# The third channel block's forward transform in 128x128 matmuls, with the whole kernel put in a new order

## Chip, core and metric

The kernel runs on one core of a Trainium2 chip. The metric is the device time of one execution in microseconds; before the change it is 645.85 us, the median of three runs (645.35 to 647.2).

## The reference

One layer of a conditioned network on 2048 tokens of 640 channels, in float32: a gated long convolution, then a wide MLP.

```python
def _A_ref(q, k, v, shift_k, ssm_k, ssm_D):
    ...                                   # k_shift: causal convolution of k with 4 taps
    kv = k_shift * v
    L = 2 * S
    kv_f = rfft(pad(kv)); kf_f = rfft(pad(ssm_k))
    y = irfft(kv_f * kf_f, L)[:S]         # long causal convolution, per channel
    y = y + kv * ssm_D
    return q * y

def _B_ref(x, w1, b1, w2, b2):
    r = relu(x @ w1 + b1)
    return (r * r) @ w2 + b2

mod = silu(c) @ w_mod                     # six rows: sa, ca, ga, sb, cb, gb
h = layernorm(x) * (1 + ca) + sa
x = x + ga * _A_ref(h, A_k, A_v, A_shift_k, A_ssm_k, A_ssm_D)
h = layernorm(x) * (1 + cb) + sb
x = x + gb * _B_ref(h, B_w1, B_b1, B_w2, B_b2)
```

(S is 2048, the MLP's inner width 1728. The names of the transforms are shortened here.)

## The kernel before

**Two halves.** The first half works through the 640 channels in five blocks of 128 (b = 0 to 4): short convolution and product k * v, the long convolution as a Fourier transform of 4096 points done by matmuls, the gate. The second half is the MLP, in four groups of 512 tokens for its first layer and eight of 256 for its second, with products split into float32r terms.

**A channel block.** `kv` (line 642) turns a tile of k and of v (groups "kt", "vt" on TensorE, the tiles kva and kvb), applies the taps and stores kv to a scratch tensor in HBM, from which `load_x` brings it back in another layout, the tile p; `load_h` brings the filter. `unit_a` (712) is the first transform, "pa": for the filter (i = 1) and for the data (i = 0), in four units (n) of eight columns of p each. `spectra` does the second step ("h" and "x", the tiles a and gb), `front` (778) multiplies the spectra, `back` (806) is the first step of the inverse transform ("qp", the table gi, the tiles wxa and wxb), and `unit_y` (831) the second ("t", transposes of q, and "y", products with cst). `prep` and `finish` are the gate and the sum. `mod_row` and `mod_col` compute rows of the conditioning ("mr"); `awake` (700) puts in twenty dummy groups of transposes ("warm").

**Two forms of the first transform.** In `unit_a` a unit is 32 products of 64x64 quarters of the array: for each of eight columns, two halves e of the partitions and two halves r of the result. They are written as two half units of 16 products. A float32 product is two weight loads and two matmuls in the trace, so a unit is 64 matmuls, and 128 instructions. `unit_a4` (736), used where (b, i) is in the set FOUR, takes all 128 partitions at once, with a table cw4 of four columns in place of two:

```python
mm(
    t[64 * r : 64 * r + 64, j].rearrange("p m d -> p (m d)"),
    pt[b][:, i, 8 * n + 4 * half + j, :],
    cw4[:, r],
    True, True, hold=[AX[b][i]],
)
```

Here a unit is 16 products, 32 matmuls and 64 instructions. Both forms fill two PSUM tiles of 128x512 in a unit, and each is copied into the tile a ("pac"), in blocks 1 to 4 by ScalarE. Before the change FOUR holds blocks 0 and 1.

**The order.** Nothing is emitted where it is written. Every step becomes a node of a graph with a key, such as ("pa", 2), and the table TURNS (1419) gives each key's nodes their due times, in hundredths of a microsecond, in the order in which they were written; `order` (179) sorts all nodes by them, and `keep_order` pins each engine to that order. The due times are a planner's; here they count as an order and nothing else. HOMES (1878) gives, by one digit a tile, which of its allowed buffers or PSUM banks a tile lives in. `sp_issue` (408) holds a transfer on SyncE's queue (SP) until the fourth one ahead of it has landed.

Of the kernel before, what the change touches and what calls it, by code (L numbers as in the profile page):

```python
# [260 lines left out]
def ssm_mlp_kernel(  # L261
# [52 lines left out]
    warm = sb.tile([P, 1], F32, tag="warm", name="warm")  # L314
# [556 lines left out]
    st2 = small("st2", (P, 2, NB, 6))  # L871
# [484 lines left out]
    def second_layer(n):  # L1356
# [46 lines left out]
        def gated(i, k, t, done=True):  # L1403
# [16 lines left out]
        ("b1", 0): [6247, 21762],  # L1420
        ("comb", 0): [4983, 5176, 5350, 5419, 5488, 5213, 5281, 5524, 5705, 5636, 5774, 6000, 6069, 6207, 6138, 6286,
            6355, 6509, 6440],
        ("comb", 1): [9572, 9677, 9608, 9503, 9856, 9787, 9719, 10175, 9949, 10244, 10313, 10454, 10689, 10892, 10824,
            11060, 10961, 11790, 11721],
        ("comb", 2): [14697, 14661, 14802, 14593, 14940, 14871, 14733, 15045, 14976, 15396, 15186, 15327, 15563,
            16040, 16309, 16788, 16423, 16492, 16719],
        ("comb", 3): [18943, 19048, 18979, 19084, 19153, 19386, 19189, 19815, 19603, 19677, 19746, 20239, 20308,
            20453, 20384, 20627, 20696, 21071, 21002],
        ("comb", 4): [23016, 23179, 23284, 22947, 23586, 23215, 23435, 23622, 24236, 23901, 24098, 24304, 24167,
# [20 lines left out]
        ("fin", 0): [13154, 15631, 13193, 14121, 12280, 12414, 13259, 13393, 11593, 12714],  # L1450
        ("fin", 1): [14229, 18629, 18157, 17429, 15841, 16312, 14429, 14923, 16109, 16243],
        ("fin", 2): [18118, 19837, 21611, 18515, 18388, 18637, 18555, 19040, 19258, 19392],
        ("fin", 3): [22111, 23723, 23079, 22071, 23970, 24104, 23691, 25536, 24712, 25085],
        ("fin", 4): [25708, 25775, 25747, 26588, 26097, 26231, 26371, 26504, 26840, 27968],
        ("gb", 0): [1955, 2141, 2424, 1791],
        ("gi", 0): [5076, 5015, 4786, 4907],
        ("h", 1): [5206, 5951, 7416, 8020, 9524, 9622, 9719, 9816, 10092, 10205, 10282, 10386, 10457, 10554, 10662,
            10945],
        ("h", 2): [12405, 12587, 12824, 13274, 14536, 14648, 14726, 14823, 14901, 14998, 15274, 15387, 15377, 15767,
            15940, 16087],  # L1460
        ("h", 3): [17094, 17387, 18492, 18624, 18928, 19026, 19154, 19251, 19359, 19467, 19762, 20038, 20248, 20369,
            20428, 20529],
        ("h", 4): [21852, 21974, 22479, 22739, 22933, 23030, 23108, 23205, 23368, 23466, 23984, 24082, 24159, 24257,
            24334, 24592],
        ("hat", 0): [25954, 26016],
        ("hat", 1): [27079, 27284],
        ("hat", 2): [27688, 27782],
        ("hat", 3): [29066, 28707],
        ("hat", 4): [34016, 34515],
        ("hat", 5): [34703, 34910],  # L1470
        ("hat", 6): [36793, 37348],
        ("hat", 7): [38305, 38447],
# [426 lines left out]
    kn = {}  # L1899
# [139 lines left out]
```

## Time and profile before

| | |
|---|---|
| timed runs | 645.35, 645.85, 647.2 us |
| profiled execution | 650.69 us, of which the span 648.9 us |
| mean granted clock of TensorE | 0.987 |
| TensorE, matmuls | 623.3 us busy |
| VectorE | 501.7 us |
| ScalarE | 363.0 us |
| GpSimd | 209.8 us |
| data moved | 111.04 MB, mean 171 GB/s |

The profile is of one execution. PE is TensorE with its matmuls, PEld its weight loads, DVE VectorE, ACT ScalarE, POOL GpSimd, SP SyncE. A row of the timeline gives start, length, engine, line, operation, the tile written and the tiles read, shapes and count, and in brackets the idle time ahead of it with what ended it. A row of a table by stretches gives the stretch and its length, then each engine's busy time and instructions, then the granted clock of TensorE, the busy share of the DMA engines and GB/s. All steps bear the line of one helper (L195), so groups are told apart by their tiles: products with cst and p are the first transform, "64*64" its quarter form and "128*64" the other. "issue" is time in which an engine waited for nothing that the profile shows.

### The profile page before, as it was taken

The page shows a single profiled execution, that of the slowest core. Times are in us where ns is not written, and L with a number is a line of the kernel's source. Part 1 is how long each engine was busy: PE and PEld are TensorE (multiplying, and loading weights), DVE is VectorE, ACT ScalarE, POOL GpSimd, SP SyncE. Part 2 cuts the span into 40 slices and gives each one's busy share as a digit, 9 for nine tenths or more (in the row PEclk, how much of TensorE's full clock was granted, in tenths as well). Part 3 has the DMA queues.
Part 4 walks back from the last instruction along what each step waited for, and adds up shares of the span by engine and source line. Part 5 has one row for each costly group of instructions (what it writes and reads, how often), then busy time and mean ns, then how long its engine had stood idle before and what let it go on. Part 6 is the DMA issues. An engine that isn't in the chain of part 4 may idle for free.

```text
span 648.9 us, 17839 instructions
## 1 busy us (share of the span) xinstructions
PE 623.3 (96%) x7268; PEld 584.2 (90%) x7268; DVE 501.7 (77%) x970; ACT 363.0 (56%) x693; POOL 209.8 (32%) x284
## 2 busy tenths in 40 slices
PE   7999889989899899999999999999999999999997
PEld 7999579859878779689999899999999999999996
DVE  2659657877779658997877696776899898789886
ACT  3674665885756673566656756457894233423331
POOL 4338437767557518312334310105320000000000
PEclk9999989999989889999999999999999999999999
DMA  9799999889779722665565643144654445463633
GB/s 226 221 263 270 256 278 210 199 212 216 189 166 223 192 80 57 169 190 173 160 191 157 181 147 106 61 142 139 204 180 155 119 128 157 140 194 94 189 112 97
DMA packets 144714, 111.04 MB, mean 171 GB/s; under 512 B 51188, under 2 KB 123700, under 8 KB 144632
## 3 DMA queue, kind: packets, MB, share of 16 engines
q1 hardware_dynamic: 142500, 109.29, 61.3%
q8 instruction: 57, 0.93, 0.6%
q10 hardware_dynamic: 2068, 0.61, 0.4%
q14 instruction: 25, 0.20, 0.1%
q0 software_dynamic: 64, 0.01, 0.0%
HBM read 79.99 MB, written 29.88 MB: 169 GB/s over the span
## 4 chain that ended last, share of the span: by engine, by line
PE 81%; DMA 7%; DVE 5%; issue 3%; ACT 2%; POOL 1%; SPq 0%; DVEq 0%; POOLq 0%
PE ps L195 81%; DMA q<-in_A_q_dram 3%; DMA wm<-in_w_mod_dram 2%; DVE kva L195 1%; DMA d<-in_A_ssm_D_dram 1%; DMA w2s<-in_B_w_dram 1%; DMA kvb<-in_A_k_dram 1%; DVE w L195 1%; DVE s L195 1%; ACT xf L195 0%; DVE xf L195 0%; POOL kacc L195 0%; DVE up L195 0%; DVE outs L195 0%; DVE kacc L195 0%
## 5 line engine op out<-in xcount | busy, mean ns | idle before, releaser
L195 PEld LDWEIGHTS ps<-a,gb 128*64 128x64 f32 x1260 | 70.0, 137 | 8.4 <-issue 4.6
L195 PE MATMUL ps<-a,gb 128*64 128x128 f32 x1260 | 76.7, 275 | 0.7 <-ACT wxa L195 0.5
L195 PE MATMUL ps<-t,w 128*128 128x256 f32 x504 | 74.8, 282 | 0.2 <-DVE t L195 0.2
L195 ACT ACTIVATE up<-ps,b1t 128x256 f32<-128x256 f32 (+1 forms) x112 | 50.3, 469 | 37.0 <-PE ps L195 35.8
L195 PEld LDWEIGHTS ps<-t,w 128*128 128x128 f32 x504 | 65.9, 188 | 0.6 <-DVE t L195 0.4
L195 PEld LDWEIGHTS ps<-cst,p 64*64 64x64 f32 (+1 forms) x2048 | 53.8, 139 | 7.8 <-issue 3.8
L195 PE MATMUL ps<-cst,p 64*64 64x64 f32 (+1 forms) x2048 | 58.2, 238 | 2.3 <-issue 1.2
L195 DVE TENSOR_TENSOR up<-ps,up 128x256 f32<-128x256 f32 (+2 forms) x74 | 33.1, 460 | 29.4 <-PE ps L195 17.8
L195 DVE TENSOR_TENSOR up<-up 128x256 f32<-128x256 f32 (+2 forms) x124 | 45.0, 385 | 7.7 <-DMA up<-h_d 6.5
L195 PE MATMUL ps<-xa,w 128*128 128x256 f32 x342 | 50.3, 282 | 0.0
L195 ACT ACTIVATE a<-ps 128x512 f32<-128x512 f32 x72 | 41.6, 626 | 14.4 <-PE ps L195 13.9
L195 PEld LDWEIGHTS ps<-xa,w 128*128 128x128 f32 x342 | 44.6, 188 | 0.0
L195 DVE SCALAR_TENSOR_TENSOR kva<-ps,tap,kva 128x511 f32<-128x511 f32 (+2 forms) x48 | 35.7, 745 | 7.7 <-ACT ktail L195 6.6
L195 PE MATMUL ps<-w,ka 128*128 128x320 f32 x216 | 40.7, 310 | 0.0
L195 PE MATMUL ps<-w,xa 128*128 128x320 f32 x216 | 40.5, 309 | 0.0
L195 ACT ACTIVATE kz<-up 128x896 fp32r<-128x896 f32 (+2 forms) x24 | 16.8, 699 | 40.2 <-DVE up L195 35.0
L195 DVE SCALAR_TENSOR_TENSOR up<-up 128x512 f32<-128x512 f32 (+3 forms) x60 | 33.7, 581 | 4.3 <-ACT up L195 4.1
L195 PE MATMUL ps<-kz,w 128*128 128x256 f32 x216 | 34.6, 281 | 0.0
L195 PE MATMUL ps<-ka,w 128*128 128x256 f32 x216 | 34.5, 283 | 0.0
L195 PEld LDWEIGHTS ps<-w,ka 128*128 128x128 f32 x216 | 34.0, 188 | 0.0
L195 PEld LDWEIGHTS ps<-w,xa 128*128 128x128 f32 x216 | 34.0, 188 | 0.0
L195 POOL TENSOR_TENSOR wm<-wm,wm 128x640 f32<-128x640 f32 x16 | 25.1, 1571 | 21.4 <-ACT wm L195 21.1
(219 smaller groups left out, 1554.8 us busy)
## 6 DMA issues: line engine op xcount, KB each, us to landing
h_d<-up SPq DMA_DIRECT2D x51, 256.0 KB, 2.9
up<-h_d SPq DMA_DIRECT2D x48, 256.0 KB, 3.4
w1s<-in_B_w_dram SPq DMA_DIRECT2D x25, 320.0 KB, 4.0
wm<-in_w_mod_dram SPq DMA_DIRECT2D x20, 320.0 KB, 4.3
p<-in_A_ssm_k_dram SPq DMA_DIRECT2D x20, 256.0 KB, 4.3
p<-kv_d SPq DMA_DIRECT2D x20, 256.0 KB, 4.6
xp<-in_A_q_dram SPq DMA_DIRECT2D x10, 512.0 KB, 6.5
xr<-x_d SPq DMA_DIRECT2D x16, 320.0 KB, 3.3
```

The costliest lines, as they stand in the source:

```text
L195: fn(*real, **{k: a.real() if isinstance(a, View) else a for k, a in kw.items()})
```

## The change

FOUR takes in block 2, so the eight units of the third block go from `unit_a` to `unit_a4`. The number of half units, PSUM tiles and copies stays; a half unit's products go from 16 to 8. Every entry of TURNS and HOMES is new, from a planner that now counts the fetches of instructions one after the other. AWAKE stays 20.

```diff
-    FOUR = {(b, i) for b in range(2) for i in range(2)}
+    FOUR = {(b, i) for b in range(3) for i in range(2)}
```

The tables of which the text speaks, in a list's order: for "pa", the eight half units of the filter and then the eight of the data.

```diff
-        ("kn", 1): [2139, 2609, 2709, 4388, 4589, 5515, 6039, 5827],
+        ("kn", 1): [2269, 3182, 3075, 4304, 4963, 5767, 5332, 5441],
-        ("kn", 2): [7639, 8690, 6548, 10064, 9434, 10708, 10881, 11464],
+        ("kn", 2): [7794, 8733, 7082, 10680, 10235, 11077, 11333, 11631],
-        ("pa", 2): [10759, 10932, 11472, 11842, 10871, 11152, 12104, 12165, 13709, 13756, 13657, 13849, 13905, 13951,
-            13346, 13398],
+        ("pa", 2): [10943, 11046, 11425, 11977, 11133, 11513, 12381, 12483, 14104, 14279, 13915, 14367, 14017, 14192,
+            13493, 13681],
-        ("pa", 3): [16801, 16847, 16130, 16191, 16692, 16754, 16238, 16285, 17620, 17682, 18085, 18131, 18280, 18341,
-            17728, 18023],
+        ("pa", 3): [17167, 17213, 16456, 16517, 16916, 17105, 16564, 16611, 17990, 18098, 18455, 18502, 18675, 18736,
+            18052, 18393],
-        ("pa", 4): [21060, 21107, 21592, 21653, 20603, 20864, 20926, 20973, 22261, 22339, 22103, 22150, 22386, 22432,
-            21700, 22041],
+        ("pa", 4): [21355, 21602, 21958, 22019, 20897, 20959, 21231, 21309, 22622, 22683, 22363, 22425, 22730, 22878,
+            22066, 22471],
-        ("qp", 3): [19505, 20039, 20664, 21153],
+        ("qp", 3): [20009, 20208, 21012, 21402],
-        ("y", 3): [21747, 22583, 23195, 24509],
+        ("y", 3): [22112, 22776, 23675, 24814],
-        ("warm", 0): [1269, 963, 1006, 1138, 788, 550, 2190, 1050, 875, 1225, 744, 657, 1312, 832, 4899, 6832, 1094,
-            919, 701, 0],
+        ("warm", 0): [1032, 1353, 813, 1412, 185, 945, 988, 682, 639, 2363, 857, 0, 529, 438, 98, 394, 351, 901, 726,
+            273],
```

More of the change, by code (lines that the diff above doesn't have):

```diff
@@ L1419, in ssm_mlp_kernel @@
     TURNS = {
[L1420 to L1426, printed above, removed]
@@ L1453, in ssm_mlp_kernel @@
[L1453 to L1460, printed above, removed]
@@ L1461, in ssm_mlp_kernel @@
[L1461 to L1470, printed above, removed]
@@ L1710, in ssm_mlp_kernel @@
-        ("mul", 4): [22850, 22782, 23011, 22943, 23175, 23244, 23586, 23751, 24063, 23994, 24241, 24173, 24448, 24379,
-            24712, 24780],
-        ("one", 0): [41842, 46562, 45749, 47344, 46344, 45900],
-        ("out", 0): [47300, 47724, 47883, 47973, 48899, 48148, 48197, 48246, 49106, 49188, 49955, 51052, 49023, 49548,
-            52643, 49636],
-        ("out", 1): [49381, 49849, 49898, 49947, 49999, 50132, 50306, 50808, 51320, 51402, 54167, 54633, 51045, 51182,
-            51366, 51446],
@@ L1717, in ssm_mlp_kernel @@
-        ("out", 2): [51219, 52060, 51652, 51701, 52242, 52193, 52559, 52692, 53174, 53448, 53582, 53536, 52741, 53366,
-            54228, 55937],
-        ("out", 3): [53453, 54213, 54123, 54262, 54429, 54629, 55189, 54762, 55457, 55540, 56341, 55846, 54811, 54997,
-            55755, 55665],
-        ("out", 4): [56041, 56477, 56295, 56344, 56526, 56693, 56742, 56924, 57506, 57588, 57912, 59608, 57124, 57729,
-            57952, 58493],
-        ("out", 5): [57834, 58673, 58034, 58083, 59490, 58249, 58624, 58575, 59578, 59744, 61295, 60482, 58831, 58955,
-            59648, 59318],
@@ L1725, in ssm_mlp_kernel @@
-        ("out", 6): [59854, 60720, 60521, 60612, 60671, 60769, 61550, 60818, 61775, 61858, 62432, 61946, 61211, 61335,
-            62392, 61691],
-        ("out", 7): [61950, 62362, 62050, 62099, 62411, 62508, 62804, 62563, 62611, 62660, 62709, 62764, 62764, 62459,
[9 rows of a table removed]
-        ("pac", 0): [1731, 1894, 1643, 1711, 1556, 2080, 1905, 1993, 4574, 4647, 4472, 4734, 4215, 4396, 4118, 4297],
-        ("pac", 1): [3668, 4094, 3608, 4154, 3729, 4847, 4275, 4336, 8761, 8821, 8882, 8954, 8640, 8700, 9129, 9190],
@@ L1774, in ssm_mlp_kernel @@
-        ("qpc", 4): [24142, 23892, 24803, 24864, 25037, 25098, 25161, 25161],
[65 rows of a table removed]
-        ("warm", 0): [1269, 963, 1006, 1138, 788, 550, 2190, 1050, 875, 1225, 744, 657, 1312, 832, 4899, 6832, 1094,
[36 rows of a table removed]
+        ("b1", 0): [6482, 21668],
+        ("comb", 0): [5201, 5407, 5269, 5338, 5581, 5512, 5443, 5981, 5912, 5774, 5843, 6049, 6118, 6187, 6256, 6404,
+            6336, 6473, 6542],
+        ("comb", 1): [9791, 9968, 9863, 9687, 10004, 10109, 10040, 10178, 10247, 10352, 10421, 11011, 10906, 11080,
+            11184, 11480, 11352, 12067, 11998],
@@ new lines, in ssm_mlp_kernel @@
+        ("comb", 2): [14785, 14922, 15132, 14853, 15201, 15063, 15237, 15306, 15375, 15479, 15584, 16630, 15991,
+            16328, 16259, 16433, 16872, 16804, 16699],
+        ("comb", 3): [19161, 19229, 19265, 19334, 19403, 19717, 19649, 19921, 19822, 19990, 20059, 20514, 20937,
+            20868, 20711, 21165, 21096, 21238, 21307],
+        ("comb", 4): [23736, 23352, 23840, 23388, 23909, 23772, 23667, 24372, 24073, 24441, 24181, 24542, 24611,
[20 rows of a table added]
+        ("fin", 0): [13444, 16133, 17040, 14298, 12417, 12872, 12875, 13624, 12673, 13767],
@@ new lines, in ssm_mlp_kernel @@
+        ("fin", 1): [14570, 18549, 17068, 17344, 16060, 16265, 14373, 15985, 16502, 16651],
+        ("fin", 2): [18850, 24181, 23907, 18958, 18487, 18885, 18997, 19403, 19521, 19655],
+        ("fin", 3): [24332, 25239, 24372, 24142, 23224, 23358, 23945, 25790, 25063, 25750],
+        ("fin", 4): [26100, 26168, 26140, 26721, 26489, 26623, 26803, 28697, 29149, 29224],
+        ("gb", 0): [1591, 1815, 2903, 2722],
+        ("gi", 0): [4969, 5029, 6358, 5338],
+        ("h", 1): [5466, 5564, 7972, 8069, 9669, 9766, 9844, 9941, 10019, 10116, 10392, 10505, 10612, 10963, 10787,
+            10902],
@@ new lines, in ssm_mlp_kernel @@
+        ("h", 2): [12804, 13544, 13303, 13665, 14853, 14959, 15037, 15134, 15212, 15309, 15592, 15698, 15775, 15872,
+            16207, 16320],
+        ("h", 3): [17464, 17826, 18887, 19000, 19308, 19421, 19498, 19596, 19732, 19923, 19921, 20261, 20547, 20675,
+            20722, 20820],
+        ("h", 4): [22217, 22328, 22940, 23071, 23317, 23423, 23500, 23598, 24187, 24300, 24377, 24474, 24552, 24649,
+            24727, 24970],
+        ("hat", 0): [26346, 26408],
+        ("hat", 1): [27456, 27450],
@@ new lines, in ssm_mlp_kernel @@
+        ("hat", 2): [28360, 28898],
+        ("hat", 3): [29086, 28992],
+        ("hat", 4): [33567, 34138],
+        ("hat", 5): [34947, 34853],
+        ("hat", 6): [37610, 37221],
+        ("hat", 7): [38868, 38727],
[50 rows of a table added]
+        ("kst", 0): [2880, 2556, 2716, 3019],
+        ("kst", 1): [4748, 6285, 7042, 7754],
+        ("kst", 2): [9725, 11488, 12347, 12737],
+        ("kst", 3): [14020, 15481, 16541, 16890],
+        ("kst", 4): [17704, 18584, 19782, 20768],
[74 rows of a table added]
+        ("lgb", 0): [986, 2160],
@@ new lines, in ssm_mlp_kernel @@
+        ("lgi", 0): [4448, 5096, 4804],
[82 rows of a table added]
+        ("lxp", 0): [10025, 7446],
+        ("lxp", 1): [10823, 11741],
+        ("lxp", 2): [14343, 14409],
+        ("lxp", 3): [18331, 18221],
+        ("lxp", 4): [20067, 20107],
[12 rows of a table added]
+        ("mul", 0): [5127, 5195, 5331, 5263, 5468, 5400, 5655, 5587, 5822, 5890, 5958, 6094, 6261, 6193, 6398, 6330],
+        ("mul", 1): [9574, 9506, 9689, 9757, 9941, 9873, 10078, 10167, 10402, 10512, 10592, 10698, 11086, 11154,
+            11835, 11692],
+        ("mul", 2): [14711, 14779, 14847, 14916, 15063, 15131, 15380, 15312, 15518, 15449, 15991, 15814, 16235, 16303,
+            16508, 16439],
@@ new lines, in ssm_mlp_kernel @@
+        ("mul", 3): [19086, 19155, 19359, 19291, 19657, 19521, 19725, 19794, 20161, 20259, 20557, 20626, 20868, 20937,
+            21096, 21164],
+        ("mul", 4): [23243, 23174, 23311, 23379, 23839, 23515, 23935, 24072, 24400, 24468, 24562, 24630, 24737, 24805,
+            25063, 25132],
+        ("one", 0): [41911, 47684, 42245, 46617, 42448, 47714],
+        ("out", 0): [48112, 48308, 48357, 48448, 49223, 48581, 48630, 48679, 49381, 49740, 51982, 51472, 49520, 49602,
+            50455, 50003],
@@ new lines, in ssm_mlp_kernel @@
+        ("out", 1): [49892, 50418, 50045, 50369, 50733, 50635, 50684, 51532, 51386, 52023, 53873, 52459, 51581, 51663,
+            53047, 51942],
+        ("out", 2): [51553, 52638, 52106, 52373, 52589, 52961, 53505, 53010, 53854, 54139, 54227, 56785, 53059, 53772,
+            57078, 54609],
+        ("out", 3): [54463, 54871, 54565, 54656, 54705, 54920, 55908, 55078, 55957, 56039, 58283, 56127, 55295, 55377,
+            56865, 57235],
+        ("out", 4): [56639, 57037, 56781, 56830, 56879, 57195, 57244, 57293, 57426, 58138, 60366, 58226, 57945, 58027,
+            58920, 58960],
@@ new lines, in ssm_mlp_kernel @@
+        ("out", 5): [58196, 59090, 58275, 58549, 58916, 59139, 60113, 59188, 60273, 60437, 60611, 60525, 59237, 60355,
+            60704, 61138],
+        ("out", 6): [60882, 61498, 61012, 61144, 61340, 61193, 61242, 61291, 62019, 62101, 63020, 62664, 61937, 62495,
+            62584, 62624],
+        ("out", 7): [62483, 62828, 62578, 62627, 62877, 62925, 62980, 63069, 63078, 63127, 63175, 63230, 63230, 63023,
[9 rows of a table added]
+        ("pac", 0): [1275, 1694, 1655, 2008, 1754, 1918, 1723, 1792, 4779, 4900, 4655, 4950, 4618, 4840, 4365, 4513],
@@ new lines, in ssm_mlp_kernel @@
+        ("pac", 1): [3871, 4106, 3522, 4381, 3609, 4260, 4046, 4321, 9155, 9216, 8983, 9068, 8862, 8923, 9276, 9337],
+        ("pac", 2): [11122, 11232, 11670, 12217, 11293, 11610, 12558, 12668, 14350, 14410, 14036, 14520, 14225, 14289,
+            13726, 13786],
+        ("pac", 3): [17270, 17330, 16608, 16779, 17177, 17391, 16669, 16839, 18155, 18376, 18558, 18697, 18818, 18879,
+            18637, 18758],
+        ("pac", 4): [21847, 21957, 22078, 22138, 21164, 21285, 21495, 21555, 22740, 22861, 22481, 22542, 22950, 23011,
+            22663, 22800],
@@ new lines, in ssm_mlp_kernel @@
+        ("pra", 0): [11979, 12277, 11183, 11421, 11471, 11353, 10704, 10876, 11073, 10852, 11869, 11451, 10753, 10803,
+            11023, 11253],
+        ("pra", 1): [13986, 12949, 13374, 13681, 15020, 15469, 14471, 14140, 13256, 12729, 12899, 13582, 12618, 12387,
+            13206, 13484],
+        ("pra", 2): [15933, 15983, 15370, 17383, 16219, 16729, 16082, 16941, 16430, 15419, 15234, 17096, 17047, 16380,
+            16032, 17245],
+        ("pra", 3): [19656, 19873, 20162, 19891, 19193, 20321, 19755, 21006, 20211, 20112, 19243, 20229, 19983, 19706,
+            20432, 20396],
@@ new lines, in ssm_mlp_kernel @@
+        ("pra", 4): [21346, 21396, 22199, 21872, 21445, 21065, 21907, 21066, 21016, 20966, 21797, 21036, 20916, 22388,
+            21115, 21691],
+        ("prm", 0): [13035, 11549, 12135, 11283],
+        ("prm", 1): [14071, 15653, 13612, 13513],
+        ("prm", 2): [17487, 16971, 18276, 17275],
+        ("prm", 3): [21622, 21803, 20327, 21464],
+        ("prm", 4): [22348, 22083, 22152, 22761],
+        ("prp", 0): [13140, 11801, 12545, 11673],
+        ("prp", 1): [14170, 15758, 13839, 13711],
@@ new lines, in ssm_mlp_kernel @@
+        ("prp", 2): [17562, 17690, 18350, 18687],
+        ("prp", 3): [21902, 22417, 20583, 23096],
+        ("prp", 4): [23457, 22221, 22545, 25473],
+        ("qp", 0): [5623, 6089, 6425, 6617],
+        ("qp", 1): [10193, 11799, 11600, 12182],
+        ("qp", 2): [15386, 15950, 16717, 17260],
+        ("qp", 3): [20009, 20208, 21012, 21402],
+        ("qp", 4): [23988, 24987, 25186, 25365],
+        ("qpc", 0): [5822, 5882, 6419, 6298, 6624, 6927, 6806, 6866],
+        ("qpc", 1): [11521, 10402, 12327, 12029, 11809, 11919, 12497, 12437],
@@ L1877, in ssm_mlp_kernel @@
+        ("qpc", 2): [15595, 15758, 16548, 16159, 16926, 16986, 17474, 17535],
+        ("qpc", 3): [20736, 20371, 20615, 20554, 21737, 21225, 21676, 21616],
+        ("qpc", 4): [24197, 25031, 25237, 25298, 25435, 25375, 25553, 25553],
[65 rows of a table added]
+        ("warm", 0): [1032, 1353, 813, 1412, 185, 945, 988, 682, 639, 2363, 857, 0, 529, 438, 98, 394, 351, 901, 726,
[36 rows of a table added]
     }
     HOMES = (
-        "0000000000000000000000000411242003501101430036112445544004466463167355010342007623052434400236417013",
-        "5332171064110723342520300110101101001010000101103121102313010130321100402133011524121310525226142440",
@@ L1886, in ssm_mlp_kernel @@
-        "0010230012301323000122334511203024530102320150132130001100110111023241305002121132010100021320102103",
-        "0121221003012120001010110101012571023147010100000120501262122140227300101101100010215010261020101000",
-        "1102370126101247021501023403120123030120101300200130200013020011000000204513630230325760410203721560",
-        "1020273150410215236471011047623051020052146710305140732102",
+        "0000000000000000000000002111215000731037210047733757331321234542156741320440306516746542050246415001",
@@ new lines, in ssm_mlp_kernel @@
+        "5302131264110703345520120110100101101110000001103123102313000132301100713273011603221362510224041400",
+        "0054101164100016011141001576070235724112020573106420320421017536030701114346210361410416230320015003",
+        "2102613112652007254010511101731110611101350050003571242360460306721043402105511172320205617010303012",
+        "45701322030730422551422641722b0112501064000127111013100161004173730402272064071046133250310356716044",
+        "200126716311300640415167020a21524912611850426b511051342304021310101710116000006701114700040110163520",
@@ new lines, in ssm_mlp_kernel @@
+        "1447050253104570210016417255230003115452010336015651230170115302304021105202614000000020013010023023",
+        "0010230012301223010102334511203024530102320150132130001100110101023241305002113132010100021320102103",
+        "0121221003012120010010110101012671023147010100000120501262122140127300011101110010215010261020101000",
+        "0102470123101264021501023403120123030120101300200130200013020011000000204513630230325760410303721560",
+        "1030273150410315236471011047623051030352146710305170632103",
```

66 lines of the change are left out of this document (removed), and 676 rows, old and new, of the table TURNS.

## Prediction

> **What bounds the kernel now.** I read the page first: its busy rows, its DMA queues and its chain.
>
> ```profile
> span 648.9 us, 17839 instructions
> ...
> PE 623.3 (96%) x7268; PEld 584.2 (90%) x7268; DVE 501.7 (77%) x970; ACT 363.0 (56%) x693; POOL 209.8 (32%) x284
> ...
> q8 instruction: 57, 0.93, 0.6%
> ...
> PE 81%; DMA 7%; DVE 5%; issue 3%; ACT 2%; POOL 1%; SPq 0%; DVEq 0%; POOLq 0%
> ```
>
> TensorE (PE) works 623.3 of 648.9 us and is 81% of the chain; no other engine comes near. So time changes here only through PE's own work, its 25.6 us of idle time, and its clock. The profiled execution took 650.69 us, 1.8 us more than its span and 4.84 us more than the median of the timed runs (645.85). I sum against 650.69 and carry the difference to the median; what that 4.84 may hide is the second rival.
>
> The row q8 matters later. Its columns are packets, MB and share: 0.93 MB in 57 packets is 16 KB a packet, and PE ran 7268 weight loads and 7268 matmuls, 14536 instructions: 255 to a packet. So q8 is PE's own program, about 256 instructions at a time.
>
> The chain between 130 and 245 us, where the third, fourth and fifth channel blocks (b = 2, 3, 4) are transformed, shows what interrupts PE:
>
> ```profile
> 140.30 3.84 PE ps L195 x186
> 144.14 1.97 issue
> 146.11 29.39 PE ps L195 x637
> 175.50 1.84 issue
> 177.35 33.15 PE ps L195 x585
> 210.50 0.00 issue
> 210.50 10.39 PE ps L195 x303
> 220.89 2.65 issue
> 223.54 16.25 PE ps L195 x381
> 239.78 0.99 issue
> ```
>
> "issue" means that PE waited for nothing that the profile shows: no semaphore, no transfer of data. Four such stops, 1.97 + 1.84 + 2.65 + 0.99 = 7.45 us. PE's timeline says what came ahead of them:
>
> ```profile
> 125.70 0.69 PE L195 MATMUL ps<-cst,p 64*64 64x64 f32 x30 [0.17 <-issue]
> ...
> 137.33 1.16 PE L195 MATMUL ps<-cst,p 64*64 64x64 f32 x64
> ...
> 140.30 3.27 PE L195 MATMUL ps<-cst,p 64*64 64x64 f32 x192 [0.35 <-DVE kva L195]
> ```
> ```profile
> 171.43 2.10 PE L195 MATMUL ps<-cst,p 64*64 64x64 f32 x128
> ...
> 216.75 2.83 PE L195 MATMUL ps<-cst,p 64*64 64x64 f32 x160
> ...
> 237.70 2.08 PE L195 MATMUL ps<-cst,p 64*64 64x64 f32 x125
> 240.78 0.33 PE L195 MATMUL ps<-cst,p 64*64 64x64 f32 x3 [0.99 <-issue]
> ```
>
> Each stop follows a burst of the quarter-tile products of the first transform. In the burst of 192 matmuls, 384 instructions with their weight loads leave in 3.27 us, so a packet of 256 lasts 2.2 us. My reading: the next packet is not there yet. It is not only a matter of other transfers in its way, for the stop of 0.99 us came with the DMA engines idle (next to last column, 0.02):
>
> ```profile
> 235.00:240.00 5.00, 4.79 (x231) 4.25 (x230) 0.68 (x1) 4.03 (x8) 1.00 0.02 4
> ```
>
> Then the clock, from the stretches around three of the stops:
>
> ```profile
> 140.00:145.00 5.00, 3.84 (x193) 3.22 (x194) 4.73 (x9) 4.40 (x9) 3.23 (x4) 1.00 0.89 226
> 145.00:150.00 5.00, 3.89 (x45) 3.18 (x46) 2.62 (x7) 1.27 (x5) 1.95 (x2) 1.00 1.05 237
> ```
> ```profile
> 175.00:180.00 5.00, 3.16 (x31) 2.51 (x28) 1.77 (x2) 1.43 (x4) 1.89 (x5) 0.84 0.84 177
> 180.00:185.00 5.00, 5.00 (x51) 3.67 (x54) 3.19 (x5) 2.70 (x6) 3.36 (x5) 0.82 0.17 34
> 220.00:225.00 5.00, 2.35 (x28) 2.16 (x26) 3.19 (x7) 1.00 (x2) 1.99 (x2) 0.78 1.01 244
> 225.00:230.00 5.00, 5.00 (x38) 4.45 (x40) 0.25 (x1) 3.06 (x6) 1.72 (x2) 0.50 0.17 41
> 230.00:235.00 5.00, 5.00 (x116) 3.92 (x109) 1.60 (x4) 2.49 (x5) 0.00 (x0) 0.70 0.74 213
> ```
>
> The third column from the right is the granted clock. After the stop at 144 it stays at 1.00; after the one at 175.5 it loses 5 x (0.16 + 0.18) = 1.7 us; after the one at 220.9 it loses 5 x (0.50 + 0.30) = 4.0 us between 225 and 235 alone. The Trainium skill (TensorE: Matmul & The Clock Gate, the section on why this matters for your kernels) asks for no idle gap over about 3 us if the clock is to stay up. By that rule neither 1.84 nor 2.65 us would have cost any clock; the trace shows that they did, and the trace decides.
>
> **The change, part by part.** *The products.* FOUR now holds block 2, so its eight units go from 64 quarter matmuls each (64x64) to 32 matmuls of 128x128. The prices:
>
> ```profile
> L195 PE MATMUL ps<-cst,p 128*64 128x128 f32 x512 | 29.2, 274 | 0.8 <-ACT we L195 0.6 <-POOL p L195 0.2
> L195 PE MATMUL ps<-cst,p 64*64 64x64 f32 x1536 | 29.0, 227 | 1.5 <-issue 1.2 <-DVE kva L195 0.3
> ```
> ```profile
> 86.73 1.97 PE L195 MATMUL ps<-cst,p 128*64 128x128 f32 x32
> ...
> 89.25 2.95 PE L195 MATMUL ps<-cst,p 128*64 128x128 f32 x50 [0.56 <-ACT we L195]
> ```
>
> In steady flow a 128x128 matmul takes (2.95 - 1.97) / 18 = 54 ns, 1.74 us for a unit of 32; a quarter one takes (3.27 - 1.16) / 128 = 16.5 ns, 1.06 us for 64. The change adds 0.68 x 8 = 5.5 us. The grouped rows give less, 29.2/16 - 29.0/24 = 0.62 a unit, 4.9 us; a unit standing alone (1.97 against 1.16) gives 0.81, 6.5 us. I take 5.5, as most units stand next to other matmuls. PE is the bound, so nothing hides it.
>
> The Trainium skill (TensorEngine Tiling (Array Packing), Available Configurations) counts four independent tiles of 64x64 in the array against two of 128x64, which would make the old form twice as fast as the new one. By that rule leaving it would cost 8 x 1.74 / 2 = 7.0 us, an estimate. The rows show 1.74 / 1.06 = 1.6 times, and the sum goes by them.
>
> *The copies out of PSUM* stay sixteen of 128x512. Those of block 1, of the 128x128 form, against those of block 2:
>
> ```profile
> L195 ACT ACTIVATE a<-ps x8: 592/597/632, 89.6 to 95.3; 128x512 f32<-128x512 f32 x8
> ```
> ```profile
> L195 ACT ACTIVATE a<-ps x16: 600/636/681, 114.1 to 144.6; 128x512 f32<-128x512 f32 x16
> ```
>
> Some 40 ns less each, on an engine that is 56% busy: nothing.
>
> *The program gets shorter*: 8 x 64 = 512 instructions fewer, two packets of 57. In block 2 a packet now lasts at least 256/64 x 1.74 = 7 us instead of 2.2. So the stop of 1.97 us and the 0.17 at 125.70 go: -2.1 us, between 0 (if another wait is late there next) and -2.1. No clock comes back here, for none was lost. Next late would be DVE's kva, which held PE for 0.35 us at 140.30.
>
> *Block 3's quarter units* keep nearly their places (in its order tables the same groups follow each other, but for one of four half units that now stands ahead of two groups of transposes), and because exactly two packets vanish ahead of them, packet boundaries fall where they did. Its stop of 1.84 us and its 1.7 us of clock stay: 0, from -3.5 to +1.
>
> *Block 4's quarter units* are spread a little. The burst of five half units (the x160 above) becomes three: one goes ahead of a group of the inverse transform, one behind another. Its second burst of four (x125 and x3) becomes three, with a group of output products ahead of the fourth. So the first burst is 64 matmuls, 64 x 16.5 ns = 1.1 us, shorter, and slower work takes their place; part of it falls into the packet before. I take 0.5 off the 2.65 and the whole 0.99: -1.5 us. Bounds: 0, and -(2.65 + 0.99 + 4.0) = -7.6 if the stop gets too short to bring the clock down.
>
> *The order and the homes anew.* From 372 us on PE is one piece:
>
> ```profile
> 372.22 269.52 PE ps L195 x2001
> ```
>
> The same products in another order take the same time there: 0. Ahead of block 2 PE waits for data here:
>
> ```profile
> 83.34 1.11 PE L195 MATMUL ps<-ident,kvb 128*128 128x128 f32 x4 [2.35 <-DMA kvb<-in_A_k_dram]
> ```
>
> In SP's order sixty transfers still stand ahead of that load, the same sixty, so its queue is neither shorter nor longer. But the second block's first load goes two transfers later, and two of the dummy groups (due 4899 and 6832) leave the stretch between the first products and the first transposes, where they filled waits. I take +0.5, from -1.5 to +2 (about that wait of 2.35 either way).
>
> Sum: 5.5 - 2.1 + 0 - 1.5 + 0.5 = +2.4 us: 653.1 for a profiled execution, 648.3 against the median.
>
> **The rivals.** *Faster: block 4's long stop falls under what halves the clock* (chance 0.34). For it: the stops at 144 (1.97) and 175.5 (1.84) lie side by side in length, one with and one without loss of clock, so the limit is near, and the 2.65 is being cut. Against: what follows it, products with one column and transposes, stays, and block 3 shows 1.84 to be enough. Then 5.5 - 2.1 - 7.6 + 0.5 = -3.7: 642.2.
>
> *Slower: the timed runs have little to give back* (0.14). The sum of stops and lost clock, 7.45 + 1.7 + 4.0 = 13 us, is of the profiled execution, which is 4.84 us longer than the timed ones. If that difference is itself in these stops, those of blocks 2 and 4 are short without the profiler, and the 5.5 us stands alone: +5.5 to +6, 651.6. It decides where the stops of blocks 2 and 4 come to under 1 us without the profiler. The Trainium skill (Runtime: NRT & Kernel Launch, Instruction fetch mechanics) points this way: it calls the crossing of a 16 KiB block of instructions mostly hidden, and gives PE room for 2048 instructions. Against it: the four stops behind quarter bursts, in a row with q8's 255 instructions to a packet.
>
> *No change* (0.12): of block 4's half clock only the stretch of 225 to 230 or that of 230 to 235 goes, 2.5 or 1.5 us, some 2 us more than in the forecast: 646.3.
>
> That the change does not do what it says I leave out: FOUR is tested at the head of unit_a.
>
> **How the numbers follow.** About 0.3% (1.9 us) is what a measurement of this kernel can tell from no change. The forecast, +2.4, has 0.40, and its own range is 646.5 to 650.5; a quarter of it, 0.10, lies under that 1.9. So slower has 0.30 + 0.14 = 0.44, the same 0.10 + 0.12 = 0.22, faster 0.34. The range goes from 640.5, halfway from the faster rival (642.2) to the case in which block 3's stop and clock go as well (642.2 - 3.5 = 638.7), to 652.5, just under the slower rival with the dear end of the products (645.85 + 6.5 + 0.5 = 652.9).
>
> **What would show it right or wrong.** Right: 1024 matmuls of 64x64 instead of 1536 and 768 of 128x128 instead of 512, the latter at 274 ns and some 44 us busy; q8 at 55 packets; no "issue" stop over 0.3 us in block 2; block 3's first stop near 1.8 us with a clock of 0.8 after it; block 4's long stop near 2 us. Wrong: if 0.50 is no longer among the clocks of block 4, the faster rival holds; if the whole stretch before block 2 shifts by more than 2 us, the new order did it and not the products; if a stop without a releaser appears in block 2 among 128x128 products, my reading of the stops is wrong.

## The result and the profile after

| | before | after |
|---|---|---|
| timed runs, median (lowest to highest), 20 each | 646.81 us (641.9 to 650.41) | 642.83 us (641.15 to 649.94) |
| ratio of the times, 95% interval | | 0.9944 (0.9923 to 0.9965) |
| profiled execution, its span | 650.69, 648.9 us | 641.7, 639.9 us |
| mean granted clock of the profiled execution | 0.987 | 0.998 |
| lost clock of the timed runs, median | 5.8 us (35 runs) | 1.3 us (20 runs) |

The kernel is 4.0 us faster, 0.56%, with an interval that leaves out no change. The last row is worked out from the span and the granted clock that each run lists: (1 - clock) x span; the 35 runs of before are those beside the first experiments. I take it as an upper measure, since over those 35 runs the time rises by only 0.65 us for each us of it. I use it below, with "the rest" for a run's time less its lost clock (the medians are taken separately).

The page of the changed kernel, its span, busy rows, clock row, the queue of TensorE's own program and the chain's shares by engine:

```profile
span 639.9 us, 17339 instructions
PE 621.5 (97%) x7012; PEld 584.2 (91%) x7012; DVE 510.4 (80%) x970; ACT 363.0 (57%) x693; POOL 208.5 (33%) x284
PEclk9999999999999999999999999999999999999999
q8 instruction: 55, 0.90, 0.6%
PE 82%; DMA 7%; DVE 6%; issue 2%; ACT 2%; POOL 1%; SPq 0%; DVEq 0%; POOLq 0%; ACTq 0%
```

PE has 256 matmuls fewer and 1.8 us less of busy time, although eight units of it now cost more. A busy time also shrinks when the clock stays up: in the kernel before, 96 quarter matmuls of block 4 took 2.84 us in the stretches at 0.50 and 0.70, and 1.63 us once the clock was back at 1.00:

```profile
229.57 2.84 PE L195 MATMUL ps<-cst,p 64*64 64x64 f32 x96
...
235.56 1.63 PE L195 MATMUL ps<-cst,p 64*64 64x64 f32 x96
```

After the change the clock row shows 9 in every slice. The idle time of PE is 639.9 - 621.5 = 18.4 us, against 25.6. What PE waited for without any releaser, before (first fence) and after:

```profile
PE ps L195 <- issue: 7.6, 5, 2.7
```
```profile
PE ps L195 <- issue: 0.4, 1, 0.4
```

Columns are total, times, longest: 7.6 us in five stops became 0.4 in one. The 7.2 us that went are the whole fall in idle time. Where the burst of 160 quarter matmuls stood in block 4, PE's timeline now shows:

```profile
214.45 1.99 PE L195 MATMUL ps<-cst,p 64*64 64x64 f32 x96
...
218.40 0.69 PE L195 MATMUL ps<-cst,p 64*64 64x64 f32 x32
...
221.17 1.63 PE L195 MATMUL ps<-cst,p 64*64 64x64 f32 x96
...
225.54 1.63 PE L195 MATMUL ps<-cst,p 64*64 64x64 f32 x96
...
228.12 1.63 PE L195 MATMUL ps<-cst,p 64*64 64x64 f32 x96
```

No run is longer than 96, and none of these rows or those between them carries a wait on "issue". The stretches of the prediction's clock tables:

```profile
140.00:145.00 5.00, 5.00 (x88) 4.65 (x82) 4.03 (x10) 4.31 (x9) 3.74 (x4) 1.00 0.44 123
175.00:180.00 5.00, 5.00 (x43) 3.58 (x43) 2.27 (x4) 2.81 (x6) 3.72 (x6) 1.00 1.02 236
220.00:225.00 5.00, 5.00 (x128) 4.14 (x127) 5.00 (x9) 4.59 (x10) 1.72 (x2) 1.00 0.81 216
225.00:230.00 5.00, 5.00 (x207) 4.41 (x208) 3.50 (x5) 3.82 (x8) 5.00 (x4) 1.00 0.47 170
230.00:235.00 5.00, 4.79 (x88) 3.56 (x84) 4.93 (x7) 3.94 (x7) 1.13 (x2) 1.00 0.01 3
```

Where before had 0.78, 0.50 and 0.70 between 220 and 235, and 0.84 behind block 3's stop, the granted clock is 1.00.

Following the start of the same groups of products through both profiled executions splits the 9.0 us: -2.2 up to the end of block 1's spectra, +1.4 over block 2, -1.8 over block 3's forward transform and -0.6 to its inverse one, -6.7 over the stretch with block 4's first bursts, -0.9 over its second ones, +1.8 from there to the end. So the faster rival's place carries the gain in the profile. One execution is a sample, though; the experiments ask what of it the timed runs show.

### The profile page after: what moved, and what is told of

Read it like the earlier page. It is cut to its first block, busy times and chain, and to the rows that moved or that the text cites. A ratio compares the mean times of both kernels' runs of the same rounds, so it can differ in the third digit from the quotient of the medians.

```text
span 639.9 us, 17339 instructions
## 1 busy us (share of the span) xinstructions
PE 621.5 (97%) x7012; PEld 584.2 (91%) x7012; DVE 510.4 (80%) x970; ACT 363.0 (57%) x693; POOL 208.5 (33%) x284
## 4 chain that ended last, share of the span: by engine, by line
PE 82%; DMA 7%; DVE 6%; issue 2%; ACT 2%; POOL 1%; SPq 0%; DVEq 0%; POOLq 0%; ACTq 0%
PE ps L195 82%; DMA kvb<-in_A_k_dram 2%; DVE up L195 1%; DMA q<-in_A_q_dram 1%; DVE kva L195 1%; DMA gi<-in_gi_dram 1%; DMA kva<-in_A_v_dram 1%; POOL wm L195 1%; DMA h_d<-up 1%; DMA p<-kv_d 1%; DMA kv_d<-kva 1%; DVE w L195 1%; DVE kacc L195 1%; ACT a L195 0%; SPq L409 0%
## 5 line engine op out<-in xcount | busy, mean ns | idle before, releaser
L195 PEld LDWEIGHTS ps<-cst,p 64*64 64x64 f32 (+1 forms) x1792 | 58.1, 136 | 7.1 <-issue 3.8
L195 PE MATMUL ps<-cst,p 64*64 64x64 f32 (+1 forms) x1792 | 62.8, 244 | 0.8 <-DMA p<-kv_d 0.7
L195 DVE TENSOR_TENSOR up<-ps,up 128x256 f32<-128x256 f32 (+2 forms) x74 | 33.2, 460 | 25.6 <-PE ps L195 14.8
```

Source lines behind the costliest of these rows:

```text
L195: fn(*real, **{k: a.real() if isinstance(a, View) else a for k, a in kw.items()})
```

## The experiments

Theory A: the gain is the splitting of block 4's bursts; the products in block 2 cost some microseconds and win back their own stop; the rest of the new order is worth nothing. Rival B: the large products of block 2 bring the gain, since two packets of instructions less move all the later stops. Rival C: the new order ahead of block 2 (the -2.2 above). In the diffs, due times are in hundredths of a microsecond, and "pac" (the copies) is moved behind the half unit that it reads. Each ratio is to the kernel before, in the runs beside it (23 to 35).

**Block 2 alone in large products**, in the order of before:

```diff
-    FOUR = {(b, i) for b in range(2) for i in range(2)}
+    FOUR = {(b, i) for b in range(3) for i in range(2)}
```

> The kernel before with FOUR alone taking in block 2; order and homes as before. If the prediction's terms hold (products 5.5 us dearer, block 2's stop of 2.1 us gone, all else as before) it is 3.4 us slower than before, and the long stops and the half clock of blocks 3 and 4 are as frequent as before. If the products themselves bring the gain it is 3 to 4 us faster than before. If the grouped rows of the two profiles price the products better (44.6 - 29.2 against 29.0 - 18.1 us for eight units, 4.5 us) it is 2.4 us slower.

Measured: 647.77 us, ratio 1.0012 (0.9984 to 1.004). Of the times expected, 3.4 us slower lies outside this interval and 2.4 us inside. The "issue" rows of its chain between 120 and 260 us, without those under 0.5 us:

```profile
177.25 1.82 issue
...
198.13 0.72 issue
...
222.33 1.43 issue
...
237.35 0.84 issue
```

The stop near 144 is gone, the three of blocks 3 and 4 stand where they stood, and one of 0.72 us stands in block 3, where the profile of before has none. Rival B falls: by itself this part gains nothing. The lost clock is 4.2 us against 5.8 and the rest 3.3 us longer, so the products are felt in part.

**The order alone**, block 2 in quarter tiles again (its third half unit had to move by a place for the memory to fit):

```diff
-    FOUR = {(b, i) for b in range(3) for i in range(2)}
+    FOUR = {(b, i) for b in range(2) for i in range(2)}
+    TURNS["pa", 2][2] = 11930
+    HOMES = homed(HOMES, {354: 7, 357: 1, 347: 7})
```

> The new order and homes with FOUR as before, so block 2 in quarter tiles (one of its half units stands next to its pair, and three tiles have another bank, since the quarter form fills both of a unit's tiles in each half). If the new order of blocks 3 and 4 brings the gain and the products cost it back in part, this is faster than the changed kernel by 1.5 to 3.4 us (640 +- 1.5), with a stop of about 2 us behind block 2's burst of six half units. If the products bring the gain it is back at 646 to 647.

Measured: 642.12 us, ratio 0.9938 (0.9909 to 0.9966), a little over the 640 +- 1.5 that was expected; the stop behind block 2's burst is back, 1.44 us. All the gain is in the order. Against 642.83 for the whole change, block 2's large products cost 0.7 us net, which is under what the runs can tell from nothing.

**The whole change with block 4's bursts put back**: three half units back in their old places, so that runs of 128 form again:

```diff
+    TURNS["pa", 4][5], TURNS["pa", 4][1], TURNS["pa", 4][13] = 21225, 21362, 22760
+    HOMES = homed(HOMES, {594: 7})
```

> The changed kernel with block 4's quarter half units in bursts of five and four again, as the kernel before had them; nothing else. If the bursts of block 4 make the long stop and take the clock down, the median is 2 to 6 us above the changed kernel's and the profile shows a stop of 2 to 3 us there, mostly with half clock behind it. If the gain came from elsewhere in the new order (the transfers, the stretch ahead of block 2), it is within 1 us of the changed kernel.

Measured: 646.08 us, ratio 1.0001 (0.9977 to 1.0025): all of the gain is gone. Timeline of PE in block 4, and its stretches:

```profile
213.75 2.12 PE L195 MATMUL ps<-cst,p 64*64 64x64 f32 x128 [0.29 <-DVE wxb L195]
...
218.11 0.94 PE L195 MATMUL ps<-gi,wxa 64*128 64x128 f32 x13 [0.93 <-issue]
...
231.23 2.09 PE L195 MATMUL ps<-cst,p 64*64 64x64 f32 x127
233.94 0.21 PE L195 MATMUL ps<-cst,p 64*64 64x64 f32 x1 [0.63 <-issue]
```
```profile
220.00:225.00 5.00, 4.53 (x99) 4.12 (x102) 2.92 (x7) 3.28 (x8) 0.44 (x1) 0.52 0.96 257
225.00:230.00 5.00, 5.00 (x136) 3.37 (x131) 1.90 (x3) 3.01 (x7) 5.00 (x4) 0.80 0.15 57
```

The first burst is of four half units here, not of the five that the expectation speaks of, and its stop is 0.93 us, not 2 to 3. It is followed all the same by a clock of 0.52 and 0.80: 5 x (0.48 + 0.20) = 3.4 us lost.

**The counterpart: before, with only those three half units spread.**

```diff
+    TURNS["pa", 4][5], TURNS["pa", 4][1], TURNS["pa", 4][13] = 20655, 21340, 22600
```

> The kernel before with three half units of block 4 moved and nothing else: the burst of five becomes three, the second burst of four becomes three and one. If block 4's bursts make the long stop, this alone is 2 to 4 us faster than before (644 to 642.5), the mirror of the 3.2 us that putting them back cost. If the gain needs the rest of the new order too, it stays within 1 us of before.

Measured: 643.46 us, ratio 0.9955 (0.9926 to 0.9983): 3.0 us gained by three half units moved, with nothing else of the change. The stops of blocks 2 and 3 are still there, with another of 0.60 us later in block 3; in block 4 only 0.2 us are left, and the clock stays:

```profile
144.81 1.53 issue
175.74 1.59 issue
...
221.02 0.21 issue
```
```profile
220.00:225.00 5.00, 4.79 (x144) 4.29 (x145) 3.05 (x8) 3.50 (x8) 3.17 (x3) 1.00 0.80 213
225.00:230.00 5.00, 5.00 (x153) 3.79 (x145) 3.27 (x7) 4.53 (x9) 0.56 (x1) 1.00 0.78 210
```

Undone, it takes the gain away; done alone, it brings three quarters of it. Theory A holds in its first part. The order alone brought 4.4 us against these 3.0, with intervals of 3.7 us each: whether the rest of the new order adds anything is not shown.

**The price of a unit**: the whole change with all five blocks in large products.

```diff
-    FOUR = {(b, i) for b in range(3) for i in range(2)}
+    FOUR = {(b, i) for b in range(5) for i in range(2)}
```

> The changed kernel with blocks 3 and 4 in 128x128 products as well: sixteen more units. No burst of quarter tiles is left. If a unit costs 0.68 us more and no stop is left to save, it is 10.9 us slower than the changed kernel (653.7); at the grouped rows' 0.56 a unit, 9.0 us (651.8). If stops of blocks 3 and 4 still cost the changed kernel several us in most timed runs, it is slower by only 4 to 7 us. The clock stays at 1.00 through blocks 2 to 4 in every execution.

Measured: 650.86 us, ratio 1.0066 (1.0041 to 1.0091), 8.0 us over the changed kernel for sixteen units more: 0.50 us each, some 0.4 to 0.6 by the two intervals. No "issue" stop over 0.2 us is left in blocks 2 to 4, so this is a price with the few stops that the changed kernel still had already taken off.

**Filler in the burst, filler in a calm stretch**: two dummy products of 128x512 (four matmuls in the trace), once inside block 4's burst of five half units, as the diff shows, once well ahead of it with due times of 19900 and 19901, both in the kernel before.

```diff
+    for i in range(2):
+        with g.as_one(1.0):
+            mm(psum(f"fill_{i}", (P, 512), ANY), ident, cst, True, True)
+    TURNS["fill", 0] = [21061, 21062]
```

> The kernel before with two dummy products of 128x512 (eight instructions, some 1.8 us of TensorE's time) put in the middle of block 4's burst of five; their result is not read, all else is as before. If the stop behind the burst is TensorE waiting for its next packet of instructions, the added work runs in the time of the stop: no slower than before by more than 0.5 us, or up to 3 us faster where the clock stays up for it. If the stop has another cause, the time grows by the added 1.8 us.

> The same two dummy products, put among block 3's spectra, where instructions are slow and no stop stands. Both theories expect the full price there: 1.8 us slower than before. It is the yardstick for the one in the burst.

Measured: in the burst 644.27 us, ratio 0.9976 (0.9946 to 1.0005); in the calm stretch 647.18 us, ratio 1.0026 (0.9999 to 1.0053). The timeline of the first:

```profile
216.69 2.14 PE L195 MATMUL ps<-cst,p 64*64 64x64 f32 x128
218.75 1.98 PE L195 MATMUL ps<-cst,ident 128*128 128x512 f32 x4
220.67 0.69 PE L195 MATMUL ps<-cst,p 64*64 64x64 f32 x32
221.29 1.16 PE L195 MATMUL ps<-gi,wxb 64*128 64x128 f32 x14
223.81 1.38 PE L195 MATMUL ps<-gi,wxb 64*128 64x128 f32 x18 [1.36 <-issue]
```

The same work of 1.98 us is at least free in the burst: 2.9 us, by the two medians, lie between the places. Each interval just takes in no change, so the sign of either is not shown; the order of the two is.

The stop has moved, too. It stands behind 14 of the 32 products with gi and wxb, in before behind 18; the stop in block 4's second burst stands behind 121 matmuls, in before behind 125; and with the filler in the calm stretch the two stand behind 14 and 121 as well. So four matmuls with their four loads, put in anywhere ahead, bring each stop four matmuls sooner, as they would the end of a packet.

**The new order up to the end of block 1 alone** (block 2 in quarter tiles; what is due later keeps before's order, with 556 added to its due times), for rival C. Two entries of the tables, against before, an early one and a late one:

```diff
-        ("kn", 1): [2139, 2609, 2709, 4388, 4589, 5515, 6039, 5827],
+        ("kn", 1): [2269, 3182, 3075, 4304, 4963, 5767, 5332, 5441],
-        ("pa", 4): [21060, 21107, 21592, 21653, 20603, 20864, 20926, 20973, 22261, 22339, 22103, 22150, 22386, 22432,
-            21700, 22041],
+        ("pa", 4): [21616, 21663, 22148, 22209, 21159, 21420, 21482, 21529, 22817, 22895, 22659, 22706, 22942, 22988, 22256, 22597],
```

> The new order and homes up to the end of block 1's spectra, the old ones from there, FOUR as before. In the two profiles the new order reaches that place 1.5 to 2.2 us earlier. If that is its work and not chance, this is 1.5 to 2 us faster than before (644.5 to 645). If it is chance of one execution, it is within 0.7 us of before.

Measured: 646.19 us, ratio 1.0003 (0.9973 to 1.0033). As the source of the whole gain rival C falls; the interval, -1.7 to +2.1 us, doesn't shut out the 1.5 us of the expectation. Its long burst is in its old place:

```profile
214.68 2.61 PE L195 MATMUL ps<-cst,p 64*64 64x64 f32 x160
220.39 1.05 PE L195 MATMUL ps<-gi,wxb 64*128 64x128 f32 x14 [1.79 <-issue]
```

It does keep the clock up at 80 to 90 us (1.00, where before has 0.78 and 0.88 behind its wait for a load), and so loses less clock over the runs, 4.5 against 7.1 us; but the rest is 1.5 us longer, and the time is the same.

**A group of output products moved into block 2's burst**, on the order alone:

```diff
+    TURNS["y", 1][3] = 14246
```

> The run with the changed order alone (four quarter-tile blocks as before, 642.12 us), with the y group of products, which stood outside block 2's burst of six half units, moved between the fourth and the fifth half unit of it. Nothing is added or left out. If it is long stretches of quarter tiles that outrun the instruction fetch, the stop of 1.44 us behind that burst goes and the kernel takes some 641 us. If the stop in block 2 comes from the fetch whatever stands between the half units, the time stays at 642 and the stop is seen again, at another place.

Measured: 642.35 us, ratio 0.9957 (0.9931 to 0.9983): no gain over the order alone (642.12). Its timeline tells why:

```profile
141.28 2.17 PE L195 MATMUL ps<-cst,p 64*64 64x64 f32 x128 [0.26 <-ACT ktail L195]
144.09 0.64 PE L195 MATMUL ps<-wxb,cst 128*64 128x512 f32 x1 [0.63 <-ACT a L195]
...
148.37 0.44 PE L195 MATMUL ps<-a,gb 128*64 128x128 f32 x4 [1.49 <-ACT a L195]
```

PE still stops, 0.63 and 1.49 us, now on ScalarE's copies into the tile a. The stop on "issue" is gone, as foretold, but another wait was next in line: 2.1 us in two pieces, where the order alone has 1.44.

**Only block 2's filter in quarter tiles**, on the whole change:

```diff
+    FOUR = {(b, i) for b in range(2) for i in range(2)} | {(2, 0)}
```

> The changed order, with block 2's filter units (four) left in quarter tiles and its data units (eight in all, half of them) in 128 by 128 products. With 0.50 us a unit from the run with all blocks in large products and no stops to lose or win, four units back in quarter tiles give 2.0 us: some 640.8 us against 642.8 of the changed kernel. If the quarter tiles pay for themselves in stops wherever they stand, the time stays between 642 and 643.

Measured: 642.35 us, ratio 0.9939 (0.9903 to 0.9976). Between 120 and 170 us its chain has one stop of 0.40 us, then 1.28 in block 3. Half a microsecond under the changed kernel and 1.5 over what was expected, both within the width of its interval (4.7 us): undecided. No run beat the changed kernel by what can be measured.

The runs by clock and rest:

| kernel | time | lost clock | rest |
|---|---|---|---|
| before (35 runs, first group; second group) | 646.5; 646.4 | 5.8; 7.1 | 640.8; 639.9 |
| after | 642.8 | 1.3 | 641.6 |
| block 2's products alone | 647.8 | 4.2 | 644.1 |
| order alone | 642.1 | 1.0 | 640.6 |
| bursts back | 646.1 | 2.6 | 644.0 |
| bursts split alone (second group) | 643.5 | 2.9 | 640.5 |
| all in large products | 650.9 | 1.6 | 649.5 |

The change lowers the lost clock by 4.5 us and leaves the rest where it was, within a microsecond. So on balance what it won is clock, but the balance hides two things: the rest holds the dearer products of block 2 as well as the stops that went, and with the bursts put back only 1.3 us of the 3.3 are lost clock, 2.4 are rest.

## Why the prediction was wrong, point by point

The prediction said 648.3, the kernel takes 642.83: +2.4 us was summed, -4.0 measured. Two steps failed. The first is the term for block 4: "I take 0.5 off the 2.65 and the whole 0.99: -1.5 us", with the 4.0 us of lost clock left standing. It measured about -3 us in the timed runs (-3.0 done alone, and 3.3 given back when undone) and -7.6 in the profiled execution (-6.7 and -0.9). The second is the pair of terms for block 2, 5.5 for the products and -2.1 for the stop, together +3.4; it measured +0.7 in the new order and +1.3 in the old one. By the medians the order was worth -4.4 against the -1.0 summed for it, and block 2 +0.7 against +3.4: 3.4 and 2.7 of the 6.4 us between sum and result.

The faster rival, put at 642.2 with a chance of 0.34, has the mechanism of block 4 right: the long stop went and the half clock with it. That its number came out as well is partly luck. It takes -7.6 for block 4, where the timed runs show some -3, and +3.4 for block 2, where they show +0.7 to +1.3.

- *Why the step for block 4 failed.* It shortened the stop by part of the products that leave the burst. But what counts is the packet, not the burst. The stops stand at the ends of packets: in the chain of before, as the prediction prints it, 637, then 585 + 303 = 888, then 381 matmuls lie between one stop and the next, which is 5, 7 and 3 times some 127, or 254 instructions with the loads, near the 256 of a packet. And TensorE stops there if it is through with a packet before the next one has come. Counted on the traces, the last 127 matmuls ahead of the stop of 2.65 us took 3.2 us; with the bursts spread (after, and bursts split alone) the packets of that stretch took 4.1 to 4.2 us, and the stop was 0.2 us or none. The length of a run by itself doesn't decide. In block 4 a stop of 0.63 us came behind 127 quarter matmuls in a row, 0.93 behind 128 and 1.79 behind 160, but 0.60 behind 96 as well (at 227 us, in the run with the output products moved), and block 3's run of 128 near 165 us is followed by none. The argument against the rival, "block 3 shows 1.84 to be enough", also assumed that a stop would remain.
- *The products* were to cost 5.5 us, bounds 4.9 to 6.5. The rows of the changed kernel give

```profile
L195 PE MATMUL ps<-cst,p 128*64 128x128 f32 x768 | 44.6, 274 | 0.7 <-DMA p<-kv_d 0.7
L195 PE MATMUL ps<-cst,p 64*64 64x64 f32 x1024 | 18.1, 221 | 0.1
```

  15.4 us more and 10.9 less than before, +4.5 in all, 0.56 a unit; the run with all blocks gives 0.50, or 4.0 for eight. The dear value came from steady flow in two rows; the grouped rows (4.9) lay nearer.
- *Block 2's stop*, -2.1: it went, as foretold. With products of 4.0, the part alone should then cost +1.9; measured +1.3 in the order of before and +0.7 in the new one. So the stop is worth 2.7 to 3.3 us in the timed runs, if the difference is all its doing, and the two terms nearly cancel instead of adding up to +3.4. Both intervals are wider than what is left.
- *Block 3*, 0 from -3.5 to +1, since its units nearly keep their places. The half unit that moves, which the prediction names and puts at nothing, cuts the burst of 128 ahead of the stop into 32 and 96; after the change:

```profile
169.07 0.69 PE L195 MATMUL ps<-cst,p 64*64 64x64 f32 x32
169.69 1.09 PE L195 MATMUL ps<-ident,kvb 128*128 128x128 f32 x8
170.72 1.63 PE L195 MATMUL ps<-cst,p 64*64 64x64 f32 x96
172.27 2.05 PE L195 MATMUL ps<-gi,wxb 64*128 64x128 f32 x31
174.74 0.37 PE L195 MATMUL ps<-gi,wxb 64*128 64x128 f32 x1 [0.42 <-issue]
```

  The stop was 0.42 here and 0.74, 0.81, 0.89 and 1.28 in four runs with the same order, against 1.59 to 1.84 in five with before's order (a sixth, with the filler in the calm stretch, has none). So the new order shortens it. The cut alone doesn't explain that, for the 127 matmuls ahead of it took 3.6 us in both; the DMA engines were 75 to 83% busy meanwhile in the new order, 90 to 97% in the old one. What it is worth in time no run shows by itself.
- *The early order*, +0.5: nothing measurable (-1.7 to +2.1 us), although the profile shows -2.2 there.
- *The rest of the program*, 0: the profile shows +1.8 between block 4 and the end, with the clock up all through. Not explained.
- *The mechanism*, that TensorE outruns the fetch of its own program in runs of quarter tiles: borne out by splitting (stop gone), rebuilding (stop back), by filler (cheap in the burst, and moving the stop by its own length in the program), and by the run with no quarter tiles at all, which has no such stop in blocks 2 to 4. The row shown for the stop of 0.99 us, 235 to 240, covers only its first 0.2 us; the next stretch, 240 to 245, shows a DMA share of 0.01, so that reading stands.
- *The slower rival* assumed that the timed runs have little to give back. They lose 5.8 to 7.1 us of clock in the median, by the same measure by which the profiled execution loses 8.4, and so had nearly as much to give.
- *What would show it wrong* named three signs. No 0.50 among the clocks of block 4, then the faster rival: that came. A shift of over 2 us ahead of block 2, then the new order: that came too (-2.2), and misleads, for the early order alone gains nothing that the timed runs show. A stop among block 2's large products, then the reading of the stops is wrong: that did not come. Of the signs that it is right, the counts, the 274 ns, q8's 55 packets and the quiet block 2 came; block 3's stop near 1.8 us with a clock of 0.8 and block 4's near 2 us did not.

What stays open is which event takes the clock down. Stops of 0.93 (bursts back), 1.43 (products alone), 1.47 (filler in the calm stretch) and 1.79 us (early order) in block 4 were followed by half clock, one of 1.36 in the same place (filler in the burst) wasn't, nor were 1.53 and 1.59 in blocks 2 and 3 (bursts split) or 1.82 in block 3 (products alone), though before's 1.84 there was. Length alone doesn't decide. In block 4 one-column products and transposes follow the stop; moving these apart was not tried. The Trainium skill (TensorE: Matmul & The Clock Gate, the section on why this matters for your kernels) puts the limit at idle gaps of about 3 us; by these rows the clock falls behind much shorter ones, and not behind all of them.

## What to carry to other kernels

When TensorE stops with no releaser, count its instructions from one stop to the next. If they come out as multiples of a packet of its program, it is through with its packets before the next ones come; spreading a few short matmuls among longer products makes the packet last longer, and cost nothing here that could be measured. Price a stop with the clock behind it, and read the clock of every timed run, for one profiled execution shows one draw: the stop of block 3 ran from 0.42 to 1.28 us over five kernels with the same order there. When a step trims a burst, ask how long the packet that ends there will last, not by how much the burst shrinks.

## What the runs showed of the hardware beyond that

- The time lost to the clock comes in equal pieces. By the rows of the stretches it is 1.7 us behind block 3's stop in before, 3.4 in block 4 with the bursts back, and 5 x (0.22 + 0.50 + 0.30) = 5.1 in block 4 of before: one, two and three times 1.7. At half clock, the 0.50 of the middle row, that is 3.4, 6.8 and 10.2 us of it. A stop of 0.93 us can come ahead of it.
- How fast the program's packets come goes with the data transfers. The 127 matmuls ahead of a stop and the stop together, counted on the traces, took 2.7 to 3.7 us at the six stops with the DMA engines at most 4% busy over these matmuls, and 3.9 to 7.4 us at all those with the engines 75% busy or more. It fits that the changed kernel goes through the packet of block 4's second burst, 122 quarter matmuls among its 127, in 3.4 us at a DMA share of 0.02 and doesn't stop. That other transfers hold the packets up is an inference; no run changed the transfers alone.
- Filler of 1.98 us of TensorE work inside a burst costs 2.9 us less than the same filler in a calm stretch.
